# Seventeen unread products, four split loads and two moved steps in the tail of an adaLN decode block

## The chip, the cores and the metric

The kernel runs on one core of a Trainium2 chip. Its metric is the device time of one execution in microseconds. A profile of one execution shows the engines TensorE (PE, with its weight loads as PEld), VectorE (DVE), ScalarE (ACT), GpSimd (POOL) and SyncE (SP, which issues the loads here).

## The reference

Two tokens (B = 2, one position each, D = 512) go through a transformer block in float32: attention over a window of 4,096 cached positions and a feed-forward layer with SiLU, both modulated by a condition c.

```python
x = A_x
mod = (_silu(c) @ w_mod).reshape(c.shape[0], 6, 1, -1)
sa, ca, ga, sb, cb, gb = (mod[:, 0], mod[:, 1], mod[:, 2], mod[:, 3], mod[:, 4], mod[:, 5])
h = _layernorm(x, axis=-1) * (1 + ca) + sa
x = x + ga * _A_ref(h, A_k_cache, A_v_cache, A_wq, A_wo)   # 32 heads, 8 kv heads, Dh 128, then @ wo
h = _layernorm(x, axis=-1) * (1 + cb) + sb
x = x + gb * _B_ref(h, B_w1, B_w2)                         # silu(h @ w1) @ w2, F = 1792
```

## The kernel before, in words

Nearly all of the work is reading: 97.5 MB of caches and weights, for two tokens. SyncE issues all large loads in one queue, in the order in which they are used: w_mod, wq, then a K and a V block of 4 MB each for the eight steps of attention (two kv heads of one token a step), then wo, w1 and w2. They go into four slots of 32 KB per partition in one large tile called `store` (the profile shows all of them under that name), and a load waits until the readers of its slot are done.

Attention (`scores`, `probabilities`, `values`) isn't touched. When it ends, `oTn` (line 443) holds the heads' outputs, turned so that they can be the weights of a product; the big matrices wo, w1 and w2 are always the moving side. Since only two tokens are computed, a product uses 32 columns of weights and writes 32 of PSUM's 128 partitions. Four such products, on the four quarters (`32 * g`), are written one after the other. A matrix row index `q` (32 of them for wo), `k` (4 for w1) or `tt` (14 for w2) stands for 128 rows of the matrix, as `load_rows` (line 402) lays them out: it loads rows `lo` to `hi` of each partition.

The tail, around which the change is made, goes like this:

- **wo** (lines 459 to 476). For rows 0 to 23, quarter `g` takes every fourth row and 512 columns ("wide"), into `acc`. The four partial sums then have to be added: `gather` (line 447) copies them to SBUF on ScalarE (`acc_o_sb`) and multiplies with `id4`. Rows 24 to 31 are "narrow": each of the four quarters takes 128 of the 512 columns of the same row, straight into `ao`. The gather stands behind row 27.
- **The second norm** (lines 477 to 495). VectorE turns `ao`, applies the gate `ga` and the residual, and sums to `ks`; a product with the constant matrix `mean512` gives the mean (`mean_b`, line 488); VectorE makes `dT`, `hT` (the weights for w1) and `vs`. The variance (`var_b`, line 509) is a product with `mean512` as well; ScalarE takes its root.
- **w1** (lines 496 to 513): 16 products of 448 columns into `hid`, row by row, the variance behind row 1.
- **SiLU** (lines 514 to 530): `hidT`, the factor `rstd`, an Exp on ScalarE, and `uT`, the weights for w2.
- **w2** (lines 531 to 552): rows 0 to 7 wide into `acc_yw`, rows 8 to 13 narrow into `acc_y`, a gather behind row 10.
- **Output** (lines 553 to 557): gate `gb`, residual, and one store.

Instructions run on each engine in the order in which a scheduler of the tile framework has put them. What is wrapped in `inorder` (line 63) keeps its place in the program; before, only the attention was wrapped. PSUM tiles come from `bank(tag, name)` (line 68): tags A, B and D have two buffers each, C and O one. A new tile in a buffer waits until those that used it are done, by semaphores.

Of the kernel before, what the change touches and what calls it, by code (L numbers as in the profile page):

```python
# [8 lines left out]
F32 = mybir.dt.float32  # L9
AF = mybir.ActivationFunctionType  # L10
# [3 lines left out]
P = 128  # L14
B, D = 2, 512
# [5 lines left out]
T2 = F // P  # L21
# [5 lines left out]
def adaln_block(  # L27
# [19 lines left out]
    nc = tc.nc  # L47
# [12 lines left out]
    once = ctx.enter_context(tc.tile_pool(name="once", bufs=1))  # L60
    psum = ctx.enter_context(tc.tile_pool(name="psum", bufs=2, space=bass.MemoryType.PSUM))
    psum1 = ctx.enter_context(tc.tile_pool(name="psum1", bufs=1, space=bass.MemoryType.PSUM))
    inorder = tc.keep_in_program_order

    def const(shape, name):
        return consts.tile(shape, F32, name=name)

    def bank(tag, name):
        return (psum1 if tag in "CO" else psum).tile([P, 512], F32, tag=tag, name=name)
# [35 lines left out]
    def summed(shape, name, pattern, axis=AX.X, **sizes):  # L105
        t = const(shape, name)
        nc.vector.tensor_reduce(t, ident.rearrange(pattern, **sizes), axis=axis, op=ALU.add)
        return t

    id4 = summed([P, 32], "id4", "p (a r) -> p r a", r=32)  # L110
# [39 lines left out]
    mean512 = const([P, P], "mean512")  # L150
# [3 lines left out]
    eps_t = const([P, 1], "eps_t")  # L154
# [4 lines left out]
    qbd = [const([P, 4, B, 4, 32], f"qbd{n}") for n in range(2)]  # L159
# [4 lines left out]
    oTn = const([P, 32, 32], "oTn")  # L164
# [3 lines left out]
    hT, uT = const([P, 4, 32], "hT_b"), const([P, T2, 32], "uT")  # L168
# [49 lines left out]
    for s0, s1, m in ((0, 2, m_a), (2, 6, m_b)):  # L218
        for k in range(4):
            v = wm[:, k].rearrange("p (s g m) -> p g s m", s=6, g=4)  # L220
            for g in range(4):
# [4 lines left out]
                    start=(k == 0),  # L226
                    stop=(k == 3),
# [10 lines left out]
    for k in range(4):  # L238
        for n in range(2):
            wv = wqt[:, k].rearrange("p (n s g m) -> p n g s m", n=2, s=4, g=G)  # L240
            for g in range(G):
# [4 lines left out]
                    start=(k == 0),  # L246
                    stop=(k == 3),
# [154 lines left out]
    def load_rows(w, per, lo, hi, s, at):  # L402
        e = w.shape[1]
        n = (hi - lo) * e
        nc.sync.dma_start(s[:, at : at + n], w.rearrange("(p q) e -> p (q e)", q=per)[:, lo * e : hi * e])
        v = s[:, at : at + n].rearrange("p (q e) -> p q e", e=e)
        return {q: v[:, q - lo, :] for q in range(lo, hi)}

    wot, w1t, w2t = {}, {}, {}
    for lo, hi, s, at in ((0, 16, 2, 0), (16, 24, 3, 0), (24, 32, 3, 4096)):  # L410
        wot |= load_rows(wo, 32, lo, hi, slot[s], at)
    for lo, hi in ((0, 2), (2, 3), (3, 4)):
        w1t |= load_rows(w1, 4, lo, hi, slot[0], lo * F)
    WIDE = 8
    for lo, hi in ((0, WIDE), (WIDE, 12), (12, 13), (13, 14)):
        w2t |= load_rows(w2, T2, lo, hi, slot[1], lo * D)

    gaT, sbT, cbT, xT = turned(ga, "gaT"), turned(sb, "sbT"), turned(cb1, "cbT"), turned(x_sp, "xT")
# [4 lines left out]
    for hp in range(HP):  # L423
# [4 lines left out]
            start=True,  # L428
            stop=True,
# [14 lines left out]
        oTn[:, :, 0:32:16], on.rearrange("p b j r -> p r b j"), axis=AX.X, op=ALU.add  # L444
    )

    def gather(acc, wide, name, start, stop):
        sb_ = once.tile([P, D], F32, tag="wide", name=name)
        nc.scalar.copy(sb_, wide)
        for g in range(4):  # L450
            nc.tensor.matmul(
                acc[32 * g : 32 * g + 32, :],
                id4,
                sb_[:, g * P : (g + 1) * P],
                start=start,
                stop=stop,
            )

    acc = bank("D", "acc_o")
    ao = bank("A", "ao")[:, :P]  # L460
    for q in range(24):
        g = q % 4
        nc.tensor.matmul(  # L463
            acc[32 * g : 32 * g + 32, :], oTn[:, q, :], wot[q], start=(q < 4), stop=(q >= 20)
        )
    for q in range(24, 32):
        for g in range(4):
            nc.tensor.matmul(  # L468
                ao[32 * g : 32 * g + 32, :],
                oTn[:, q, :],  # L470
                wot[q][:, g * P : (g + 1) * P],
                start=(q == 24),
                stop=(q == 31),
            )
        if q == 27:
            gather(ao, acc, "acc_o_sb", False, False)
    aoT = once.tile([P, 4, 32], F32, tag="aoT", name="aoT")
    nc.vector.transpose(aoT, ao.rearrange("p (m k) -> p k m", k=4))  # L478
    x1T = once.tile([P, 4, B], F32, tag="x1T", name="x1T")
# [5 lines left out]
    ks = once.tile([P, B], F32, tag="ks", name="ks")  # L485
    nc.vector.tensor_reduce(ks, x1T.rearrange("p k b -> p b k"), axis=AX.X, op=ALU.add)
    mean = bank("B", "mean_b")
    nc.tensor.matmul(mean[:, :B], mean512, ks, start=True, stop=True)
    dT = once.tile([P, 4, B], F32, tag="dT", name="dT")
    nc.vector.tensor_sub(dT, x1T, mean[:, None, :B].to_broadcast([P, 4, B]))  # L490
    nc.vector.tensor_mul(hT[:, :, 0:32:16], dT, cbT[:, :, 0:32:16])  # L491
# [2 lines left out]
    vs = once.tile([P, B], F32, tag="vs", name="vs")  # L494
    nc.vector.tensor_reduce(vs, sq.rearrange("p k b -> p b k"), axis=AX.X, op=ALU.add)
    FC = F // 4
    hp = bank("A", "hid")[:, :FC]
    for k in range(4):
        for g in range(4):
            nc.tensor.matmul(  # L500
                hp[32 * g : 32 * g + 32, :],
                hT[:, k, :],
                w1t[k][:, g * FC : (g + 1) * FC],
                start=(k == 0),
                stop=(k == 3),
            )
        if k == 1:
            var = bank("B", "var_b")
            nc.tensor.matmul(var[:, :B], mean512, vs, start=True, stop=True)
            std = once.tile([P, B], F32, tag="stdb", name="std_b")  # L510
            nc.scalar.activation(std, var[:, :B], AF.Sqrt, bias=eps_t)
            rstd = once.tile([P, B], F32, tag="rstdb", name="rstd_b")
            nc.vector.reciprocal(rstd, std)
    ax = once.tile([P, P], F32, tag="ax", name="ax")
    nc.vector.tensor_mul(ax, ao, ga)
    nc.vector.tensor_add(x1, x_sp, ax)
# [13 lines left out]
    nc.vector.tensor_mul(uT[:, :, 0:32:16], z, sg)  # L530
    yw = bank("D", "acc_yw")
    for tt in range(WIDE):
        g = tt % 4
        nc.tensor.matmul(  # L534
            yw[32 * g : 32 * g + 32, :],
            uT[:, tt, :],
            w2t[tt],
            start=(tt < 4),
            stop=(tt >= WIDE - 4),
        )  # L540
    y = bank("D", "acc_y")[:, :P]
    for tt in range(WIDE, T2):
        for g in range(4):
            nc.tensor.matmul(
                y[32 * g : 32 * g + 32, :],
                uT[:, tt, :],
                w2t[tt][:, g * P : (g + 1) * P],
                start=(tt == WIDE),
                stop=(tt == T2 - 1),
            )  # L550
        if tt == 10:
            gather(y, yw, "acc_y_sb", False, False)
    yo = once.tile([P, P], F32, tag="yo", name="yo")
    nc.vector.tensor_mul(yo, y, gb)
    nc.vector.tensor_add(yo, yo, x1)
# [29 lines left out]
```

## Time and profile before

| | |
|---|---|
| time, median of 3 runs | 238.48 us (238.08 to 238.54) |
| time of the profiled execution | 238.67 us |
| its span, first to last instruction | 236.9 us |
| TensorE busy | 143.4 us (61%) |
| VectorE busy | 113.1 us (48%) |
| ScalarE busy | 28.8 us (12%) |
| mean granted TensorE clock | 0.827 |
| HBM read | 97.53 MB, 412 GB/s over the span |

The profile is of one execution, with times from the start of its span. The chain of waits follows the work that ended last back from the end, at each step to what released it. The timeline gives start, length and kind of merged pieces of one engine, and in brackets how long the engine had been idle and what ended that. Shapes are partitions x elements; "128*32" is the weights' shape. A float32 product shows as two TensorE records. The windows view gives, for each stretch, its length, the busy time of PE, PEld, DVE, ACT and POOL (with the number of records), TensorE's granted clock (1.00 is full), the share of the load engines that was busy, and GB/s.

### The profile page before, as it was taken

What the parts mean: (1) busy time and instruction counts of PE and PEld (TensorE: products, weight loads), DVE (VectorE), ACT (ScalarE), POOL (GpSimd) and SP (SyncE); (2) the same over time, 40 slices, a digit from 0 to 9 for tenths busy, and PEclk for the clock granted to TensorE, in tenths of its full rate; (3) what the DMA queues carried; (4) which work ended last, traced back from release to release, by engine and by line L of the source; (5) the groups of instructions that cost most, each with busy time, mean ns of one, the idle gap of its engine ahead of it and who ended that gap; (6) DMA issues with size and microseconds to landing.
All of it is one profiled execution on the core that took longest, in us unless ns stands there. A gap on an engine that the chain in (4) does not pass through costs nothing.

```text
span 236.9 us, 2420 instructions
## 1 busy us (share of the span) xinstructions
PE 143.4 (61%) x1012; PEld 40.2 (17%) x1012; DVE 113.1 (48%) x155; ACT 28.8 (12%) x64; POOL 7.1 (3%) x27
## 2 busy tenths in 40 slices
PE   0005954638167866887375747737746597736954
PEld 0003211110010211222101200200220222205212
DVE  0125110478497793995394396377449410102130
ACT  2010000010310120111201200300210112030200
POOL 5004000100000000000000000000000000000000
PEclk9999996756957797797979976977997869996579
DMA  7999999999999999999999999999999999999970
GB/s 266 466 421 443 437 418 421 437 415 437 443 433 443 434 409 437 415 429 443 437 432 443 412 437 421 426 443 434 427 437 426 432 423 426 418 421 413 437 300 3
DMA packets 4222, 97.68 MB, mean 412 GB/s; under 512 B 476, under 2 KB 500, under 8 KB 1012
## 3 DMA queue, kind: packets, MB, share of 16 engines
q1 hardware_dynamic: 4188, 97.52, 96.3%
q8 instruction: 8, 0.13, 0.2%
q14 instruction: 2, 0.02, 0.0%
q10 hardware_dynamic: 24, 0.01, 0.0%
HBM read 97.53 MB, written 0.00 MB: 412 GB/s over the span
## 4 chain that ended last, share of the span: by engine, by line
DMA 53%; DVE 24%; PE 12%; issue 6%; ACT 2%; SPq 0%; POOL 0%; ACTq 0%; POOLq 0%
DMA store<-in_A_k_cache_dram 25%; DVE kT L287 17%; DMA store<-in_A_wq_dram 16%; DMA store<-in_A_wo_dram 12%; PE hid L500 2%; PE q L242 2%; PE s L292 2%; DVE store L329 2%; PE acc_yw L534 2%; PE ao L468 1%; ACT store L322 1%; DVE store L327 1%; DVE mx L300 1%; DVE qT L253 1%; ACT L322 1%
## 5 line engine op out<-in xcount | busy, mean ns | idle before, releaser
L287 DVE STREAM_TRANSPOSE kT<-store 128x2048 f32<-128x2048 f32 x32 | 71.1, 2280 | 15.6 <-DMA store<-in_A_k_cache_dram 15.6
L292 PE MATMUL s<-kT,qbd 128*32 128x512 f32 x256 | 48.5, 840 | 31.0 <-DVE kT L287 31.0
L355 PE MATMUL o<-store 128*32 128x512 f32 x256 | 36.8, 725 | 1.0 <-ACT store L345 1.0
L292 PEld LDWEIGHTS s<-kT,qbd 128*32 128x32 f32 x256 | 6.4, 125 | 67.7 <-DVE kT L287 66.9
L242 PE MATMUL q<-store,hq_T 128*32 128x512 f32 x64 | 9.8, 765 | 5.9 <-DMA store<-in_A_wq_dram 5.9
L355 PEld LDWEIGHTS o<-store 128*32 128x32 f32 x256 | 9.3, 129 | 21.4 <-issue 19.8
L327 DVE STREAM_TRANSPOSE store<-store 128x512 f32<-128x512 f32 x8 | 5.7, 711 | 13.5 <-ACT store L322 13.5
L321 ACT COPY bias<-bp 128x1 f32<-128x1 f32 x8 | 1.3, 160 | 89.1 <-PE bp L319 89.1
L187 PE MATMUL mean_a<-mv_a,avg 128*128 128x1 f32 x2 | 0.6, 362 | 18.8 <-DVE avg L112 18.8
L300 DVE TENSOR_REDUCE mx<-s 128x1 f32<-128x512 f32 x8 | 5.5, 692 | 11.2 <-PE s L292 11.2
L329 DVE TENSOR_TENSOR store<-store,half 128x512 f32<-128x512 f32 x16 | 10.4, 689 | 0.2
L336 PE MATMUL pT<-store,sel 128*32 128x256 f32 x64 | 7.5, 414 | 4.5 <-DVE store L329 4.5
L365 PE MATMUL o_all<-store,pick 128*32 128x256 f32 x32 | 7.7, 382 | 2.9 <-ACT store L362 2.9
L362 ACT COPY store<-o 128x512 f32<-128x512 f32 x8 | 4.7, 587 | 31.0 <-PE o L355 31.0
L345 ACT ACTIVATE store<-pT,par 128x256 f32<-128x256 f32 x16 | 6.7, 475 | 10.8 <-PE pT L336 10.8
L253 DVE STREAM_TRANSPOSE qT<-q 128x512 f32<-128x512 f32 x2 | 1.4, 718 | 13.3 <-PE q L242 13.0
L463 PE MATMUL acc_o<-store,oTn 128*32 128x512 f32 x48 | 5.6, 595 | 2.8 <-DMA store<-in_A_wo_dram 2.8
L302 PE MATMUL mT<-ident,mx 128*1 128x128 f32 x16 | 3.0, 270 | 6.5 <-DVE mx L300 6.5
L478 DVE STREAM_TRANSPOSE aoT<-ao 128x128 f32<-128x128 f32 x1 | 0.3, 318 | 13.6 <-PE ao L468 13.6
L438 DVE TENSOR_TENSOR on<-o_all,rq 128x256 f32<-128x256 f32 x1 | 0.4, 425 | 12.3 <-PE o_all L365 12.3
L319 PE MATMUL bp<-negscale,mrow 1*128 1x1 f32 x16 | 3.1, 261 | 5.1 <-DVE mrow L314 5.1
L500 PE MATMUL hid<-store,hT_b 128*32 128x448 f32 x32 | 5.8, 865 | 0.5 <-DVE hT_b L491 0.5
(121 smaller groups left out, 92.9 us busy)
## 6 DMA issues: line engine op xcount, KB each, us to landing
store<-in_A_k_cache_dram SPq DMA_DIRECT2D x8, 4096.0 KB, 29.9
store<-in_A_v_cache_dram SPq DMA_DIRECT2D x8, 4096.0 KB, 28.4
store<-in_A_wq_dram SPq DMA_DIRECT2D x2, 4096.0 KB, 31.8
store<-in_w_mod_dram SPq DMA_DIRECT2D x1, 6144.0 KB, 17.2
store<-in_A_wo_dram SPq DMA_DIRECT2D x1, 4096.0 KB, 32.6
store<-in_A_wo_dram SPq DMA_DIRECT2D x2, 2048.0 KB, 25.1
store<-in_B_w_dram SPq DMA_DIRECT2D x1, 2048.0 KB, 29.1
store<-in_B_w_dram SPq DMA_DIRECT2D x1, 1792.0 KB, 26.2
```

The costliest lines, as they stand in the source:

```text
L242: nc.tensor.matmul(q_ps[n][32 * g : 32 * g + 32, :], hq_T[:, k, :], wv[:, n, g], start=(k == 0), stop=(k == 3),)
L287: inorder(nc.vector.transpose(kT, kv[:, :, j, :]))
L292: inorder(nc.tensor.matmul(s_ps[r : r + 32, :], qbd[h // 4][:, h % 4, b, j, :], kT[:, 32 * f : 32 * f + 32, u:32:2], start=(j == 0), stop= ...
L300: inorder(nc.vector.tensor_reduce(mx, s_ps, axis=AX.X, op=ALU.max))
L327: inorder(nc.vector.transpose(xp, pr))
L329: inorder(nc.vector.tensor_mul(zp[:, 32 * f : 32 * f + 32, :].rearrange("p (s y) w -> p s y w", y=2), xp[:, :, None, 0:16].to_broadcast([P ...
L336: inorder(nc.tensor.matmul(tp[32 * a : 32 * a + 32, :], sel, zp[:, :, 4 * a : 4 * a + 4], start=True, stop=True,))
L345: inorder(nc.scalar.activation(pt[:, :, u, :], tp.rearrange("p (n g) -> p n g", g=G), AF.Copy, scale=par[:, u : u + 1],))
L355: inorder(nc.tensor.matmul(o_ps[32 * c_ : 32 * c_ + 32, :], ptb[t % 2][:, 32 * i : 32 * i + 32], vt[t][:, 512 * i : 512 * i + 512], start= ...
L365: inorder(nc.tensor.matmul(o_all[32 * hp : 32 * hp + 32, :, :], pick[:, n].rearrange("p w i -> p (w i)"), ob[:, :, n, :], start=(n == 0), ...
L463: nc.tensor.matmul(acc[32 * g : 32 * g + 32, :], oTn[:, q, :], wot[q], start=(q < 4), stop=(q >= 20))
L500: nc.tensor.matmul(hp[32 * g : 32 * g + 32, :], hT[:, k, :], w1t[k][:, g * FC : (g + 1) * FC], start=(k == 0), stop=(k == 3),)
```

## The change

Four things are changed, all in the tail.

1. wo's rows 24 to 31 come in two loads instead of one (24 to 27 and 28 to 31), and so do w2's rows 0 to 7 (0 to 3 and 4 to 7).
2. wo's gather stands ahead of rows 28 to 31 in the written order (`copied`, then `narrow` with `id4`), and w2's stands ahead of all the narrow rows. The variance's product with what ScalarE and VectorE make of it stands ahead of w1's first row.
3. `fill(n)` issues n products of `mean512` (128 x 128) with 512 columns of `qbd[0]`, left over from attention, into tiles named "unread" in bank C, which nothing reads: three ahead of wo's rows 28 to 31, two behind them, one behind the mean, three ahead of w1's row 0, two behind its row 2, five behind its row 3, one ahead of w2's gather.
4. All products of the tail go through `product`, which keeps them in program order.

```diff
-    for lo, hi, s, at in ((0, 16, 2, 0), (16, 24, 3, 0), (24, 32, 3, 4096)):
+    for lo, hi, s, at in ((0, 16, 2, 0), (16, 24, 3, 0), (24, 28, 3, 4096), (28, 32, 3, 6144)):
...
-    for lo, hi in ((0, WIDE), (WIDE, 12), (12, 13), (13, 14)):
+    for lo, hi in ((0, 4), (4, WIDE), (WIDE, 12), (12, 13), (13, 14)):
...
+    idle_w = qbd[0].rearrange("p s b j c -> p (s b j c)")[:, :D]
+
+    def fill(n):
+        for _ in range(n):
+            inorder(nc.tensor.matmul(bank("C", "unread"), mean512, idle_w, start=True, stop=True))
+
+    def product(acc, w, rows, g, n, start, stop):
+        inorder(nc.tensor.matmul(
+            acc[32 * g : 32 * g + 32, :n], w, rows, start=start, stop=stop
+        ))
+
+    def narrow(acc, w, rows, start, stop):
         for g in range(4):
...
+            product(acc, w, rows[:, g * P : (g + 1) * P], g, P, start, stop)
+
+    def copied(wide, name):
+        t = once.tile([P, D], F32, tag="wide", name=name)
+        nc.scalar.copy(t, wide)
+        return t
...
     for q in range(24):
...
+        product(acc, oTn[:, q, :], wot[q], q % 4, D, q < 4, q >= 20)
+    acc_sb = copied(acc, "acc_o_sb")
+    for q in range(24, 28):
+        narrow(ao, oTn[:, q, :], wot[q], q == 24, False)
+    narrow(ao, id4, acc_sb, False, False)
+    fill(3)
+    for q in range(28, 32):
+        narrow(ao, oTn[:, q, :], wot[q], False, q == 31)
+    fill(2)
...
-    nc.tensor.matmul(mean[:, :B], mean512, ks, start=True, stop=True)
+    inorder(nc.tensor.matmul(mean[:, :B], mean512, ks, start=True, stop=True))
+    fill(1)
...
+    var = bank("B", "var_b")
+    inorder(nc.tensor.matmul(var[:, :B], mean512, vs, start=True, stop=True))
...
+    fill(3)
     hp = bank("A", "hid")[:, :FC]
     for k in range(4):
         for g in range(4):
...
+            product(hp, hT[:, k, :], w1t[k][:, g * FC : (g + 1) * FC], g, FC, k == 0, k == 3)
+        if k == 2:
+            fill(2)
+    fill(5)
...
     for tt in range(WIDE):
...
+        product(yw, uT[:, tt, :], w2t[tt], tt % 4, D, tt < 4, tt >= WIDE - 4)
+    yw_sb = copied(yw, "acc_y_sb")
     y = bank("D", "acc_y")[:, :P]
+    fill(1)
+    narrow(y, id4, yw_sb, True, False)
     for tt in range(WIDE, T2):
...
+        narrow(y, uT[:, tt, :], w2t[tt], False, tt == T2 - 1)
```

More of the change, by code (lines that the diff above doesn't have):

```diff
@@ L445, in adaln_block @@
     )
-    def gather(acc, wide, name, start, stop):
-        sb_ = once.tile([P, D], F32, tag="wide", name=name)
-        nc.scalar.copy(sb_, wide)
-        for g in range(4):
[L451 to L457, printed above, removed]
+    idle_w = qbd[0].rearrange("p s b j c -> p (s b j c)")[:, :D]
[7 more added lines that the diff above has]
+    def narrow(acc, w, rows, start, stop):
+        for g in range(4):
+            product(acc, w, rows[:, g * P : (g + 1) * P], g, P, start, stop)
[3 more added lines that the diff above has]
+        return t
     acc = bank("D", "acc_o")
@@ L461, in adaln_block @@
     for q in range(24):
[L462 to L476, printed above, removed]
+        product(acc, oTn[:, q, :], wot[q], q % 4, D, q < 4, q >= 20)
[7 more added lines that the diff above has]
+    fill(2)
     aoT = once.tile([P, 4, 32], F32, tag="aoT", name="aoT")
@@ L496, in adaln_block @@
     FC = F // 4
+    var = bank("B", "var_b")
+    inorder(nc.tensor.matmul(var[:, :B], mean512, vs, start=True, stop=True))
+    std = once.tile([P, B], F32, tag="stdb", name="std_b")
+    nc.scalar.activation(std, var[:, :B], AF.Sqrt, bias=eps_t)
+    rstd = once.tile([P, B], F32, tag="rstdb", name="rstd_b")
+    nc.vector.reciprocal(rstd, std)
+    fill(3)
     hp = bank("A", "hid")[:, :FC]
@@ L499, in adaln_block @@
         for g in range(4):
[L500 to L513, printed above, removed]
+            product(hp, hT[:, k, :], w1t[k][:, g * FC : (g + 1) * FC], g, FC, k == 0, k == 3)
+        if k == 2:
+            fill(2)
+    fill(5)
     ax = once.tile([P, P], F32, tag="ax", name="ax")
@@ L532, in adaln_block @@
     for tt in range(WIDE):
[L533 to L540, printed above, removed]
+        product(yw, uT[:, tt, :], w2t[tt], tt % 4, D, tt < 4, tt >= WIDE - 4)
+    yw_sb = copied(yw, "acc_y_sb")
     y = bank("D", "acc_y")[:, :P]
+    fill(1)
+    narrow(y, id4, yw_sb, True, False)
     for tt in range(WIDE, T2):
[L543 to L552, printed above, removed]
+        narrow(y, uT[:, tt, :], w2t[tt], False, tt == T2 - 1)
     yo = once.tile([P, P], F32, tag="yo", name="yo")
```

## The prediction

> **What bounds the kernel now.** I read the chain of waits first. Until 213.7 us it is the loads: caches and weights come in at 412 GB/s over the span, and the change touches nothing of that. The question is the tail. Its rows in the chain (start, length, what):
>
> ```profile
> 213.78 1.25 PE ao L468 x32
> 215.03 0.43 PE ao L451 x8
> 215.46 1.73 PE ao L468 x32
> ...
> 218.32 0.04 issue
> 218.36 0.60 PE mean_b L488 x2
> ...
> 219.41 3.22 PE hid L500 x16
> 222.63 0.52 PE var_b L509 x2
> 223.15 2.52 PE hid L500 x16
> ...
> 227.85 0.22 DVE uT L530
> ...
> 228.16 3.65 PE acc_yw L534 x16
> ...
> 231.89 0.59 ACT acc_y_sb L449
> ...
> 232.53 0.43 PE acc_y L451 x8
> 232.96 0.70 PE acc_y L544 x24
> ...
> 233.68 0.30 DVE yo L554
> ```
>
> TensorE and VectorE hand over to each other from 213.78 to the first yo at 233.68. What follows (the second yo, the store, the end) is unchanged; so whatever moves the start of yo moves the span. The windows view, cut where the clock changes, gives TensorE's clock (the seventh column, the share granted) beside its busy time:
>
> ```profile
> 207.73:211.15 3.42, 1.92 (x16) 0.50 (x16) 0.00 (x0) 0.14 (x1) 0.00 (x0) 1.00 0.97 412
> 211.15:214.56 3.41, 0.78 (x28) 0.78 (x32) 0.00 (x0) 1.73 (x2) 0.00 (x0) 1.00 1.02 432
> 214.56:217.97 3.41, 2.61 (x52) 2.15 (x44) 0.76 (x5) 0.00 (x0) 0.00 (x0) 0.50 0.96 400
> 221.39:224.80 3.41, 3.41 (x22) 1.09 (x18) 0.17 (x1) 1.54 (x2) 0.00 (x0) 0.50 1.01 428
> 228.22:231.63 3.41, 3.41 (x20) 1.05 (x24) 0.00 (x0) 0.00 (x0) 0.00 (x0) 0.50 0.42 160
> ```
>
> The clock changes only in steps of 3.41 us. A stretch with 1.92 us of work left it full, one with 0.78 us dropped it to half for the next, one with 2.61 us did not raise it, a full one did. So hid and acc_yw, the two large groups of the tail, run at half clock. Last, when the weights land (the SP queue's issues, and each one's time to landing):
>
> ```profile
> 184.14 29.60 DMA store<-in_A_wo_dram
> 191.80 0.33 SPq L405 DMA_DIRECT2D store<-in_B_w_dram  x1
> store<-in_B_w_dram SPq DMA_DIRECT2D x1, 1792.0 KB, 26.2
> 198.16 0.33 SPq L405 DMA_DIRECT2D store<-in_B_w_dram  x1
> store<-in_B_w_dram SPq DMA_DIRECT2D x1, 2048.0 KB, 29.1
> 208.90 0.33 SPq L405 DMA_DIRECT2D store<-in_B_w_dram  x1
> store<-in_B_w_dram SPq DMA_DIRECT2D x1, 256.0 KB, 22.1
> ```
>
> wo's last rows land at 213.74, w1's first two at 218.0, w2's first eight at 227.26, its last row at 231.0. So two limits lie near each other: TensorE ends at 233.65, and no change to the tail's work can end it before about 231.4 (231.0, four narrow products, a tail of 0.2). At most some 2.2 us are to be had.
>
> **The change part by part: the price of an unread product.** It is a float32 product of 128 x 512 on all 128 rows of PSUM, which before does not have. Nearest rows:
>
> ```profile
> 204.08 3.64 PE L463 MATMUL acc_o<-store,oTn 128*32 128x512 f32 x32 [1.59 <-DMA store<-in_A_wo_dram]
> 208.97 1.92 PE L463 MATMUL acc_o<-store,oTn 128*32 128x512 f32 x16 [1.26 <-DMA store<-in_A_wo_dram]
> 200.57 1.91 PE L365 MATMUL o_all<-store,pick 128*32 128x256 f32 x8 [0.76 <-ACT store L362]
> 194.52 0.65 PE L336 MATMUL pT<-store,sel 128*32 128x256 f32 x8
> 45.59 0.49 PE L261 MATMUL qr<-qg,rep 128*128 128x128 f32 x2 [0.65 <-POOL qg L257]
> ```
>
> All are at full clock; a product is two records. acc_o's 16 and 8 products differ by 1.72 us, so eight cost 1.72 us, 0.215 each, and 0.20 is the tail of a group. But they write four different quarters of PSUM in turn and run side by side. o_all's four products of 256 columns all write the same 32 rows, so they cannot: (1.91 - 0.20)/4 = 0.43 us each. pT's four of 256 columns, on four quarters, take 0.65 - 0.20 = 0.45 us together. One alone takes as long as four side by side; an unread product fills all four quarters by itself, so for 512 columns it costs 2 x 0.43 = 0.86 us. Bounds: 0.215 (as if it shared the array) and 0.86; I take 0.86, since o_all is the row where nothing overlaps. The Trainium skill has a figure that speaks for less: its page "TensorE: Matmul & The Clock Gate", section "Back-to-back issue gap", gives about 131 ns as the sustained spacing of 512-column matmuls, and "FP8 and Floating Point Precision", section "TensorE Precision Notes", counts four passes for true FP32, which makes an estimated 0.52 us; the o_all row disagrees.
>
> Then the wait. All unread products write the same one-buffer bank C, and in the new order each waits for TensorE's own semaphore. On TensorE before, from wo's narrow rows to the mean, then the same place now (id_91 is the gather's weight, mean_115 the constant matrix mean512):
>
> ```order
> L468 MATMUL ao<-store,oTn 32x128 [waits DMAHW7_49]
> L468 MATMUL ao<-store,oTn 32x128 x15
> L451 MATMUL ao<-acc_o_sb,id_91 32x128 [waits Activation_49]
> L451 MATMUL ao<-acc_o_sb,id_91 32x128 x3
> L468 MATMUL ao<-store,oTn 32x128 x16
> L488 MATMUL mean_b<-ks,mean_115 128x2 [waits DVE_49]
> ```
>
> ```order
> L455 MATMUL ao<-acc_o_sb,id_91 32x128 [waits Activation_49]
> L455 MATMUL ao<-acc_o_sb,id_91 32x128 x3
> L452 MATMUL unread<-qbd_125,mean_115 128x512 [waits PE_49] x3
> L455 MATMUL ao<-store,oTn 32x128 [waits DMAHW0_49]
> L455 MATMUL ao<-store,oTn 32x128 x15
> L452 MATMUL unread<-qbd_125,mean_115 128x512 [waits PE_49] x2
> L491 MATMUL mean_b<-ks,mean_115 128x2 [waits DVE_49]
> ```
>
> The gather moved ahead of the second half of the rows, which now wait for a load of their own, and five unread products stand ahead of the mean. The second and later ones of a group wait until the one before is out of the array. The qr row prices that from an empty start: 0.49 us for 128 columns, of which 0.86/4 = 0.215 is streaming, so 0.275 is start and drain; with 0.04 us from a signal to the next start (the issue row at 218.32) 0.315. Bounds: nothing, and the mean's whole 0.60 us, at half clock; qr is nearest in shape and clock. So the first of a group costs 0.86, each further one 1.17; a group of three 3.20, of two 2.03, of five 5.54. All queue in order on TensorE: whatever stands behind them waits.
>
> Now the queue, at full clock throughout: TensorE is never idle long enough, in any 3.41 us, to fall under the 1.92 us that kept it full. wo's rows 24 to 27 land halfway between the two starts 208.97 and 213.78, at 211.38; their 16 narrow products are four times 0.215, 0.86: 212.24. The gather, whose copy I leave where it was, takes 0.21: 212.45. Three unread: 215.65, which is 1.87 past the landing of rows 28 to 31. Those: 216.51, and with the tail 216.71, where before ended at 217.19: 0.48 gained by earlier work and clock. From ao's end to the mean's start VectorE took 1.17 us (217.19 to 218.36), so the mean could start at 217.88. What VectorE did next before:
>
> ```profile
> 218.99 0.16 DVE L490 TENSOR_TENSOR dT<-x1T,mean_b 128x8 f32<-128x8 f32 x1 [0.68 <-PE mean_b L488]
> 219.47 0.16 DVE L495 TENSOR_REDUCE vs<-sq 128x2 f32<-128x8 f32 x1
> ```
>
> But two unread hold TensorE until 218.54. The mean, about 0.3 at full clock (0.28 to 0.60), gives dT at 218.87, 0.12 earlier than before. So the gain is gone here. One unread: 218.69 to 219.55; vs, 0.64 after dT's start, is ready at 219.51; the variance is queued by 219.70. Three unread: 222.90, while hT is ready and w1's first two rows have been there since 218.0. On TensorE before, then now, from there to acc_yw:
>
> ```order
> L500 MATMUL hid<-store,hT_b 32x448 [waits DMAHW0_49,DVE_49]
> L500 MATMUL hid<-store,hT_b 32x448 x7
> L509 MATMUL var_b<-vs,mean_115 128x2 [waits DVE_49]
> L500 MATMUL hid<-store,hT_b 32x448 [waits DMAHW1_49]
> L500 MATMUL hid<-store,hT_b 32x448 x3
> L500 MATMUL hid<-store,hT_b 32x448 [waits DMAHW2_49]
> L500 MATMUL hid<-store,hT_b 32x448 x3
> L534 MATMUL acc_yw<-store,uT 32x512 [waits DMAHW3_49,DVE_49,PE_49]
> ```
>
> ```order
> L502 MATMUL var_b<-vs,mean_115 128x2 [waits DVE_49]
> L452 MATMUL unread<-qbd_125,mean_115 128x512 [waits PE_49] x3
> L455 MATMUL hid<-store,hT_b 32x448 [waits DMAHW1_49]
> L455 MATMUL hid<-store,hT_b 32x448 x7
> L455 MATMUL hid<-store,hT_b 32x448 [waits DMAHW2_49]
> L455 MATMUL hid<-store,hT_b 32x448 x3
> L452 MATMUL unread<-qbd_125,mean_115 128x512 [waits PE_49] x2
> L455 MATMUL hid<-store,hT_b 32x448 [waits DMAHW3_49]
> L455 MATMUL hid<-store,hT_b 32x448 x3
> L452 MATMUL unread<-qbd_125,mean_115 128x512 [waits PE_49] x5
> L455 MATMUL acc_yw<-store,uT 32x512 [waits DMAHW4_49,DVE_49]
> ```
>
> The variance left hid's middle, and ten unread products stand ahead of acc_yw. A hid product at full clock is 0.215 x 448/512 = 0.188. Twelve: 225.16. Two unread: 227.19. Four: 227.94, tail 228.14; before 225.67, so 2.47 late, although hid itself takes 3.0 instead of 5.7. From hid's end to uT VectorE and ScalarE take 2.40 (225.67 to 228.07): uT at 230.54. But five unread last until 233.48, 2.9 past uT. acc_yw, 1.72 and tail, ends at 235.40 instead of 231.81. The copy with its gaps: 236.07; the one unread there ends at 236.06 and is hidden. The gather and 24 narrow products, 0.21 + 1.29 + 0.20: 237.77, yo at 237.80. That is 4.1 us later than 233.68.
>
> The moved variance saves nothing: its Sqrt, table load and rstd end long before hid. The loads: two more issues on SP, each 0.33, and as completion counters are shared in turn, w2's later loads wait in the new program for wo's to land, the last until 213.74. That costs nothing: the load queue ahead of it is then still 17 us long (231.0). If splitting slows the rows, bounded by one issue each, 0.3 us either way, that is covered since acc_yw starts after the last row has landed. The profiled execution took 238.67, 0.19 over the median of 238.48; 4.1 more gives 242.8 for it and **242.6** for a median.
>
> **The rivals.** First, the products fit the gaps: faster. If an unread product streams in 0.43, half my price, then by the same steps (0.74 with the wait) ks is ready before the mean's turn, hid ends at 224.05, uT is ready at 226.45, acc_yw ends at 229.16, and yo waits for w2's last row: 231.56, 2.1 earlier, 236.4. Between the two prices the time moves 6.2 us for 0.43, so the sides change at 0.58 a product. For it: half clock really does cost hid and acc_yw some 5 us before. Against it: the o_all row. By the skill's 0.52 it would be about 0.8 us faster. That the products do not run at all is in this case too: rows and clock alone gain about the same; the order speaks against it. Chance 0.06.
>
> Second, the wait costs nothing, because TensorE overlaps start and drain in spite of the semaphore. With 0.86 for each product the same steps give hid's end at 226.28, acc_yw's at 232.30, yo at 234.69: 1.0 later, 239.5. For it: acc_o's products hide all but one tail; against it: those have no wait between them. Chance 0.14.
>
> Third, the clock falls to half in spite of it all, since with waits the products stream only 0.86 of 1.17, 73%, and 2.61 of 3.41 (77%) did not raise it before. Then every later product doubles, 10 us or more: over 250. Against it: 1.92 of 3.41 kept it full, and it is full when they start. Chance 0.04.
>
> **How the numbers follow.** My forecast has 0.72: TensorE's queue becomes the bound. Prices between the first two rivals that cancel out: 0.04. A measurement can tell about 0.2%, 0.5 us. So faster 0.06, same 0.04, slower 0.72 + 0.14 + 0.04 = 0.90. The range goes down to the second rival, 239.4. Upward, if each of the ten waits costs 0.5 (most of the mean's 0.60), 1.9 more: 244.5. That leaves out the first rival, the third and some edges, under 2 in 10.
>
> **What would show it.** Right: TensorE's clock 1.00 from 211 to the end, unread products about 1.17 us apart, the mean, hid and acc_yw each released by TensorE's own queue and not by VectorE or a load, uT ready almost 3 us before acc_yw starts, yo near 237.8. Wrong: unread products 0.5 us apart, or acc_yw starting when uT or w2's rows arrive.

## The result, and the profile after

The changed kernel takes 245.31 us (median of 6 runs, 245.23 to 245.83), the kernel before 238.25 us (6 runs, 237.91 to 238.54): a ratio of 1.0301, with a 95% interval of 1.0287 to 1.0315. It is 7.1 us slower; forecast were 242.6 us and at most 244.5. The profiled execution took 245.29 us, with a span of 243.5. Its yo starts at 240.05 instead of 233.68, 6.37 us later; the forecast had 237.80.

The chain of waits, from the landing of wo's rows 24 to 27 on (start, length, what):

```profile
211.39 1.30 PE ao L455 x40
212.69 1.07 PE unread L452 x2
213.76 0.04 issue
213.80 1.14 PE unread L452 x2
214.94 0.04 issue
214.99 1.12 PE unread L452 x2
216.11 1.01 PE ao L455 x32
...
219.36 0.12 PE mean_b L491 x2
219.48 1.07 PE unread L452 x2
...
224.10 2.39 PE hid L455 x24
...
228.73 0.89 PE hid L455 x8
...
235.41 1.85 PE acc_yw L455 x16
...
240.05 0.30 DVE yo L542
```

From 211.39 to 240.03 there is nothing but TensorE in it: no load, and neither VectorE nor ScalarE. The unread products follow each other 1.19 us apart (213.80, 214.99), each released by the one before. VectorE has its part ready long before it is wanted; from its timeline, ks and uT:

```profile
218.12 0.16 DVE L489 TENSOR_REDUCE ks<-x1T 128x2 f32<-128x8 f32 x1
231.85 0.20 DVE L531 TENSOR_TENSOR uT<-z,sgh 128x28 f32<-128x28 f32 x1
```

The mean starts about 1.1 us after ks, acc_yw 3.4 us after uT. The windows view (length, busy time by engine, the clock in the seventh column):

```profile
204.50:207.60 3.10, 3.10 (x20) 1.09 (x16) 0.00 (x0) 0.00 (x0) 0.00 (x0) 0.50 0.98 418
211.40:229.50 18.10, 17.75 (x130) 6.68 (x130) 1.79 (x11) 3.27 (x4) 0.00 (x0) 1.00 0.99 411
229.50:235.30 5.80, 5.57 (x14) 1.49 (x10) 1.94 (x7) 0.23 (x1) 0.00 (x0) 1.00 0.09 36
```

The clock is full from 211.40 on, to the end: hid takes 2.39 + 0.89 us where it took 5.7, acc_yw 1.85 where it took 3.65. The price is that TensorE works almost without a pause (17.75 of 18.10 us), and still does so when the loads have ended (36 GB/s in the last row).

### The profile page after: what moved, and what is told of

It reads as the page before. It is cut to its first block, busy times and chain, and to the rows that moved or that the text cites. A ratio compares the mean times of both kernels' runs of the same rounds, so it can differ in the third digit from the quotient of the medians.

```text
span 243.5 us, 2490 instructions
## 1 busy us (share of the span) xinstructions
PE 153.6 (63%) x1046; PEld 42.6 (18%) x1046; DVE 113.2 (46%) x155; ACT 28.8 (12%) x64; POOL 7.1 (3%) x27
## 4 chain that ended last, share of the span: by engine, by line
DMA 60%; DVE 17%; PE 15%; issue 5%; ACT 1%; SPq 0%; POOL 0%; POOLq 0%
DMA store<-in_A_k_cache_dram 34%; DMA store<-in_A_wq_dram 15%; DVE kT L287 14%; DMA store<-in_A_wo_dram 11%; PE unread L452 8%; PE q L242 2%; PE hid L455 1%; PE ao L455 1%; PE acc_yw L455 1%; PE acc_y L455 1%; DVE qT L253 1%; DVE store L329 1%; ACT L322 1%; PE s L292 0%; DVE qbd L267 0%
## 5 line engine op out<-in xcount | busy, mean ns | idle before, releaser
L292 PE MATMUL s<-kT,qbd 128*32 128x512 f32 x256 | 47.8, 823 | 33.2 <-DVE kT L287 33.2
L355 PE MATMUL o<-store 128*32 128x512 f32 x256 | 33.6, 670 | 1.0 <-ACT store L345 1.0
L452 PE MATMUL unread<-qbd,mean 128*128 128x512 f32 x34 | 19.1, 645 | 0.6
L355 PEld LDWEIGHTS o<-store 128*32 128x32 f32 x256 | 8.7, 122 | 19.2 <-issue 17.6
L455 PE MATMUL acc_o<-store,oTn 128*32 128x512 f32 x48 | 7.1, 750 | 3.2 <-DMA store<-in_A_wo_dram 3.2
L452 PEld LDWEIGHTS unread<-qbd,mean 128*128 128x128 f32 x34 | 5.1, 188 | 11.6 <-PE unread L452 8.9
```

What stands on the lines that cost most here:

```text
L292: inorder(nc.tensor.matmul(s_ps[r : r + 32, :], qbd[h // 4][:, h % 4, b, j, :], kT[:, 32 * f : 32 * f + 32, u:32:2], start=(j == 0), stop= ...
L355: inorder(nc.tensor.matmul(o_ps[32 * c_ : 32 * c_ + 32, :], ptb[t % 2][:, 32 * i : 32 * i + 32], vt[t][:, 512 * i : 512 * i + 512], start= ...
L452: inorder(nc.tensor.matmul(bank("C", "unread"), mean512, idle_w, start=True, stop=True))
L455: inorder(nc.tensor.matmul(acc[32 * g : 32 * g + 32, :n], w, rows, start=start, stop=stop))
```

## The experiments

Three sets on three chips, each beside runs of the kernel before on its own chip. Ratios are against those, with a 95% interval; they compare all times of a run, so they are not the ratios of the medians. Only the changed kernel differs from the kernel before by more than 2%. Where a smaller difference is called faster or slower below, it is because its interval leaves out 1.

**e1_none, without the unread products.** This kernel leaves out all seventeen.

```diff
     def fill(n):
-        for _ in range(n):
-            inorder(nc.tensor.matmul(bank("C", "unread"), mean512, idle_w, start=True, stop=True))
+        return
```

> The changed kernel without the seventeen unread products; loads, order and everything that is read are unchanged. Theory (the products, queued on TensorE, are the whole loss): wo's rows 28 to 31 start when they land at 213.8, hid waits for w1 at 218.0 and runs partly at half clock, and yo waits for w2's last rows: 236.1 to 237.0 us, 1.2 to 2.1 faster than before. Rival (split loads, shared completion counters or the new order lose time too): 238.3 us or more.

237.76 us (237.14 to 239.31), ratio 0.9982 (0.9960 to 1.0004). The whole loss is gone, so it lies in the unread products; against the kernel before, loads and order together lose nothing. But the gain is smaller than either figure of the theory, and the times spread over 2.2 us. The profiled execution (237.38 us) shows why there was little to gain. Its chain:

```profile
218.11 5.37 PE hid L454 x32
...
225.98 3.55 PE acc_yw L454 x16
...
232.05 0.30 DVE yo L541
```

ao is done 2.2 us earlier, hid starts when w1 lands, but both large groups run at half clock for most of their time, as before.

**e2_group, without the waits.**

```diff
-        for _ in range(n):
-            inorder(nc.tensor.matmul(bank("C", "unread"), mean512, idle_w, start=True, stop=True))
+        t = bank("C", "unread")
+        for i in range(n):
+            inorder(nc.tensor.matmul(t, mean512, idle_w, start=i == 0, stop=i == n - 1))
```

> As changed, but the unread products of one place are one accumulation in one tile, so that only the first of a group waits. Theory (a further product pays 0.32 us for draining and refilling the array): ten waits fewer, 3.2 us less than the change, 242.1 us. Rival (the wait costs nothing, the product itself is 1.18 us long): 245.3 us as before the experiment.

242.12 us (242.06 to 242.20), ratio 1.0151 (1.0119 to 1.0182): the theory to 0.02 us. Its chain has each group in one piece:

```profile
212.84 2.77 PE unread L453 x6
215.61 1.01 PE ao L456 x32
216.62 1.91 PE unread L453 x4
218.54 0.12 PE mean_b L492 x2
...
227.82 4.49 PE unread L453 x10
232.31 1.85 PE acc_yw L456 x16
...
236.95 0.30 DVE yo L543
```

Three products take 2.77, five 4.49: 0.86 for each further one, as priced from o_all, and a remainder of 0.2 in every group. yo starts 3.10 us earlier than with the waits, although wo's rows 24 to 27 landed 0.15 later in this execution: from that landing on it is 3.25, ten waits of 0.325.

**e3_half, half as many columns, waits kept.**

```diff
-            inorder(nc.tensor.matmul(bank("C", "unread"), mean512, idle_w, start=True, stop=True))
+            inorder(nc.tensor.matmul(bank("C", "unread")[:, :256], mean512, idle_w[:, :256], start=True, stop=True))
```

> As changed, but each unread product has 256 columns instead of 512; the waits stay. Theory (0.86 us of streaming, by columns, plus 0.32 us for a wait): 0.43 us less for each; 0.75 with a wait; the queue still ends about with before: yo near 233.5, 238.1 us. Rival (the cost is mostly fixed per product, not by columns): over 242 us.

238.62 us (238.53 to 238.74), ratio 1.0007 (0.9990 to 1.0024). The products are paid by columns: by its chain, unread products with a wait start 0.76 us apart instead of 1.19. The time is 0.5 us over the theory, but not because of TensorE's queue: yo starts at 233.34 in its profile, 0.16 ahead of the 233.5 expected. The theory added 4.6 us from yo's start to the whole time, and here it is 5.26, as in the changed kernel (5.24). All twelve times lie within 0.21 us, while 26 runs of the kernel before on that chip spread from 237.60 to 239.24.

**e4_loads, the split loads alone, in the kernel before.**

```diff
-    for lo, hi, s, at in ((0, 16, 2, 0), (16, 24, 3, 0), (24, 32, 3, 4096)):
+    for lo, hi, s, at in ((0, 16, 2, 0), (16, 24, 3, 0), (24, 28, 3, 4096), (28, 32, 3, 6144)):
...
-    for lo, hi in ((0, WIDE), (WIDE, 12), (12, 13), (13, 14)):
+    for lo, hi in ((0, 4), (4, WIDE), (WIDE, 12), (12, 13), (13, 14)):
```

> The kernel before with the two load splits alone. Theory (the splits cost nothing and let half of wo's last rows and the gather run before the others land): ao done near 214.9 instead of 217.2, hid starts with w1 at 218.0 instead of 219.4: about 1.4 us faster than before, 236.8 us. Rival (smaller loads and shared counters slow the queue): 238.3 us or more.

237.28 us (237.16 to 237.59), ratio 0.9945 (0.9926 to 0.9964): faster, by 1.0 to the median beside it. Here the scheduler put the variance ahead of hid by itself, and wo's gather between the two halves of the narrow rows, where it had been all along. So of the moved steps only w2's gather was a move beyond what the loads bring. Its chain shows what ends it now:

```profile
208.94 21.02 DMA store<-in_B_w_dram
...
230.09 1.07 PE acc_y L544 x24
...
232.10 0.30 DVE yo L554
```

hid (5.95 us) and acc_yw (3.22 us) still run long here, but acc_yw ends at 229.90 and isn't in the chain any more: the last step waits for w2's rows 8 to 11, which land at 229.96. On the same chip e4 is 0.5 us below e1_none by the median, and its times spread over 0.4 us instead of 2.2, though yo starts at the same point in both profiles (232.10 and 232.05). In e1_none acc_yw, the copy and the gather stand ahead of all narrow rows and are in the chain; that this makes its executions longer is not shown.

**e5_bridge, two unread products alone, behind hid.** The group of e2, everywhere else left out.

```diff
-    fill(3)
...
-    fill(2)
...
-    fill(1)
...
-    fill(3)
...
-        if k == 2:
-            fill(2)
-    fill(5)
+    fill(2)
...
-    fill(1)
```

> The changed kernel's loads and order, with two unread products, as one group, behind hid alone; the other fifteen are left out. Theory (only the gap from hid to uT, 2.5 us in the run without unread products, costs clock: acc_yw took 3.55 us there and would take 1.9): the group ends before uT, acc_yw ends when w2's row 7 has landed plus 1 us, yo near 231.5 instead of 232.05: 236.8 us. Rival (the loads' end leaves nothing to gain, or two products do not hold the clock): 237.3 us or more.

236.98 us (236.88 to 237.16), ratio 0.9957 (0.9941 to 0.9974). From its timeline, the group and the products behind it, which run at full clock (1.00 from 223.30 to 229.00):

```profile
223.31 1.98 PE L453 MATMUL unread<-qbd,mean 128*128 128x512 f32 x4
225.92 1.07 PE L456 MATMUL acc_yw<-store,uT 128*32 128x512 f32 x8 [0.62 <-DVE uT L526]
227.40 1.07 PE L456 MATMUL acc_yw<-store,uT 128*32 128x512 f32 x8 [0.41 <-DMA store<-in_B_w_dram]
229.88 1.70 PE L456 MATMUL acc_y<-store,uT 128*32 128x128 f32 x48 [0.23 <-DMA store<-in_B_w_dram]
231.65 0.29 DVE L536 TENSOR_TENSOR yo<-acc_y,mod_sp 128x128 f32<-128x128 f32 x1 [5.83 <-PE acc_y L456]
```

The group ends 0.6 us before acc_yw may start, acc_yw waits for its own rows, and yo starts 0.40 us earlier than in e1_none's profile. Its w2's last row was issued at 213.8 and landed 17.3 us later, at 231.1, 0.55 us before yo; in e8 below that distance is 0.54. So this is the loads' end. That the two products make the kernel faster than the same loads and order without them isn't shown by the times: the interval overlaps that of e1_none, which ran on another chip. Nor is any run with unread products shown to be faster than e4_loads, which has none (0.9945).

**e6_quarter, the grouped products on narrow weights.**

```diff
-        for _ in range(n):
-            inorder(nc.tensor.matmul(bank("C", "unread"), mean512, idle_w, start=True, stop=True))
+        t = bank("C", "unread")[:, :512]
+        for i in range(n):
+            for g in range(4):
+                product(t, id4, idle_w[:, :512], g, 512, i == 0, i == n - 1)
```

> As the grouped run, but each unread product of 128 columns of weights becomes four of 32 (id4), on the four quarters, side by side: the same 0.86 us of streaming. Theory (what was still missing in the sum, about 2.3 us, is the change between weights of 128 and of 32 columns, 0.2 us into a group and 0.15 us out of it): 239.8 us. Rival (any new group or tile costs it, whatever the width): 242.1 us as the grouped run.

240.78 us (240.72 to 240.92), ratio 1.0116 (1.0093 to 1.0139), between the two. The chain answers line by line to that of e2:

```profile
212.74 2.58 PE unread L457 x24
215.32 0.87 PE ao L457 x32
216.19 1.72 PE unread L457 x16
217.91 0.31 PE mean_b L493 x2
218.22 0.99 PE unread L457 x8
...
226.97 4.29 PE unread L457 x40
231.26 1.72 PE acc_yw L457 x16
...
235.54 0.30 DVE yo L544
```

Now the groups that follow narrow weights take 0.86 a product, and ao and acc_yw after them 0.14 and 0.13 less: the change of width is what cost 0.2 into a group and 0.14 out of it. It isn't any new group or tile, since these are new too. The mean, whose weights are 128 wide, became 0.19 longer in exchange, and so did the variance, and the groups behind these two still pay 0.13 for the way back (0.99 for one product). That is the larger part of why 1.41 us is saved in yo and not 2.3; 0.10 of the 1.41 is that wo's rows landed earlier than in e2. A product on 128 columns of weights also fills all four quarters at once, and e6 changes both together; what in the array takes the time is not shown.

**e7_small and e8_fit, products that fit the gaps.** e7 is e2 with 128 columns, e8 is e6 with 256.

```diff
-        t = bank("C", "unread")
+        t = bank("C", "unread")[:, :128]
...
-            inorder(nc.tensor.matmul(t, mean512, idle_w, start=i == 0, stop=i == n - 1))
+            inorder(nc.tensor.matmul(t, mean512, idle_w[:, :128], start=i == 0, stop=i == n - 1))
```

> As the grouped run, but with 128 columns for 512 in each unread product: 0.215 us of streaming. Theory (groups of 1.0, 0.8, 0.55, 1.0, 0.8 and 1.4 us fit into the gaps, and TensorE keeps full clock): yo waits for w2's last row, 231.4 to 231.7: 236.7 us, with little spread. Rival (so few columns do not hold the clock): 237.3 to 237.8 us with the spread of the run without unread products.

> As the quarter-wide run, but with 256 columns: 0.43 us for four side by side, no wait, no change of width. Theory (at half the price the seventeen fit the gaps, as the first rival of the prediction had it, and w2's last row ends the kernel): 236.7 us, 1.6 us faster than before, with little spread. Rival (TensorE's queue is still too long somewhere): 238 us or more.

e7: 237.03 us (236.84 to 237.53), ratio 0.9959 (0.9942 to 0.9977). e8: 237.15 us (236.96 to 237.29), ratio 0.9968 (0.9952 to 0.9984). Both are faster, as the theory has it, by 0.7 and 0.6 us to the median beside them (237.77). But only e8 keeps TensorE at full clock in the tail: in e7's profile it is at half from 218.24 to 221.65, and hid's first twelve products take 4.07 us, without moving the end. e8's chain ends on w2's last row:

```profile
213.87 17.45 DMA store<-in_B_w_dram
...
231.37 0.47 PE acc_y L457 x8
...
231.86 0.30 DVE yo L544
```

So products at half the price fit the gaps, as the first rival of the prediction had it, when they wait for nothing and stay quarter-wide. At half the price with waits and full-width weights e3 had yo at 233.34 and not at 231.56: the rival's sum, which has the waits, leaves out the same term as the forecast, and the price of 0.58 at which the sides were to change is too high, since e3 at 0.43 is the same as before.

**e9_one_w2 and e10_one_wo, e5 with one of the splits undone.**

```diff
-    for lo, hi in ((0, 4), (4, WIDE), (WIDE, 12), (12, 13), (13, 14)):
+    for lo, hi in ((0, WIDE), (WIDE, 12), (12, 13), (13, 14)):
```

```diff
-    for lo, hi, s, at in ((0, 16, 2, 0), (16, 24, 3, 0), (24, 28, 3, 4096), (28, 32, 3, 6144)):
+    for lo, hi, s, at in ((0, 16, 2, 0), (16, 24, 3, 0), (24, 32, 3, 4096)):
```

> As the run with two unread products behind hid, but w2's rows 0 to 7 in one load, as before the change. Theory (w2's split buys nothing, since rows 4 to 7 land at 227.4 in either case and acc_yw at full clock then takes 1.9 us, ahead of row 8's landing at 229.8 plus what w2's last row needs): 236.7 to 237.0 us, the same or 0.2 us faster, by w2's last row landing at 231.0 instead of 231.2. Rival (the split matters): 237.3 us or more.

> As the run with two unread products behind hid, but wo's rows 24 to 31 in one load, as before the change. Theory (wo's split is what the change has of use: it takes half of the narrow rows and the gather, 1.2 us at full clock, out of the way before the last rows land): ao, the mean and hid 1.2 us or more later, 237.5 to 238.5 us, with the spread of the kernel before, whose clock hangs on where the 3.41 us steps fall. Rival (hid waits for w1 and the end for w2 in any case): 237.0 us.

Both theories fell. e9: 237.41 us (237.13 to 239.64), ratio 0.9982 (0.9955 to 1.0008). e10: 237.11 us (236.79 to 237.78), ratio 0.9951 (0.9931 to 0.9970). wo's split isn't needed for the gain. w2's is worth some 0.3 us to the median of e9 against e10, 0.39 in yo. Without it the gain is only unclear, not gone: nine of e9's twelve times lie below every time of the kernel before on that chip (237.57 and more), three lie between 238.78 and 239.64, and why is not shown. In e9's timeline acc_yw has to wait for all eight rows at once:

```profile
225.79 0.21 DVE L526 TENSOR_TENSOR uT<-z,sgh 128x28 f32<-128x28 f32 x1
227.59 1.92 PE L456 MATMUL acc_yw<-store,uT 128*32 128x512 f32 x16 [2.13 <-DMA store<-in_B_w_dram]
```

and the copy, the gather and 24 narrow products come behind it, to 232.05. I had compared acc_yw's end with a landing and left out what still follows. In e10's profile ao is 2.4 us later than in e5's, but hid, which in e5 had to wait for w1's rows and ran most of its first twelve products at half clock, runs through in 3.52 us and ends at the same time.

## Why the prediction was wrong in size, point by point

**The bound: right.** TensorE's queue became the bound, and the mean, hid and acc_yw were each released by it. That nothing before 231.4 was to be had was right as well: the best yo of all runs is e5's 231.65.

**An unread product streams for 0.86 us: right,** by e2 and e6 (0.86 each) and by e3 (paid by columns). The estimate of 0.52 us, worked out in the prediction from the 131 ns that the Trainium skill's page "TensorE: Matmul & The Clock Gate", section "Back-to-back issue gap", gives for 512 columns, is not borne out by these runs.

**A waited product pays 0.315 us more: right.** They stood 1.19 us apart against 1.17, and taking ten waits away moved yo by 3.10 against 3.15 (3.25 from the landing of wo's rows on). The second rival is out.

**"So the first of a group costs 0.86": this step failed.** A group of one took 1.07 us. The seven groups took 19.26 us by the chain against 17.72, 0.2 too much in each; the quarter-wide groups behind them (ao, hid twice, acc_yw) 0.55 more than priced. That is 2.1 of the 2.25 us that are missing in yo. The rest is the first ao group with its gather, 1.30 us for a price of 1.07 that left out the 0.20 of a group's tail, less 0.06 at the mean and the variance. The last of the seven was to be hidden behind the copy, but ended 0.35 us after it. The prices came from rows in which the width of the weights never changes (acc_o, o_all, pT) or from a product into an idle array (qr), and I put them side by side without a term for the change. e6 shows that it goes with the width. The range failed with it: its upper end stretched only the waits. Of the 2.7 us between 242.6 and 245.31, the other 0.45 is not in the tail's work: 0.25 lies behind yo's start (5.24 us to the end of the time against 4.99 in the profile before), where I had expected no change, and 0.19 was taken off the forecast because the profiled execution before was that much over its median, which after it is not (245.29).

**The clock: right where it counted.** It was full from 211.40 to the end, as forecast. Before that, from 204.50 to 207.60, it was at half, which the sum doesn't contain, but acc_o still ended at 211.14, before wo's next rows landed at 211.35. The third rival, 73% of streaming being too little to hold the clock, is out. The measure behind the forecast, that 1.92 us of work in 3.41 keep it full, does not hold in general: e7 lost it after 2.43 us.

**The gather moved: wrong, without a consequence.** The order quoted in the prediction shows wo's gather between the two halves already; only the load they wait for changed.

**The loads cost nothing: right.** By e4 they even gain 1.0 us, and by the ratios no kernel with unread products gains more. In the changed kernel that gain is buried: split up by the runs, yo is 1.82 us earlier with products that fit (e8 against before), 3.68 later by the full length (e6 against e8), 1.41 by the changes of width that e6 takes away (e2 against e6) and 3.10 by the waits (the changed kernel against e2), which makes the 6.37. The terms are taken from single executions on different chips, whose landings differ by up to 0.15 us.

That the kernel before spreads (236.8 to 239.4 in the three sets) because the clock's steps fall differently on its gaps is argued, not shown: the runs whose tail has no gap spread little (e2 0.14 us, e3 0.21), but each profile is of one execution, and the mean granted clock of the whole execution doesn't go with its time in any of the three sets.

## What to carry to other kernels

Work put into a gap to keep TensorE's clock up has to be priced like any other: columns at the rate of a group that cannot run side by side, the drain where a one-buffer tile makes each product wait for the last, and the change to another width of weights on both sides. Make such a group shorter than the gap, as one accumulation; two products in the one gap ahead of the last large group did as well here as seventeen small ones. But the two split loads without any unread product (e4) did as well as either, since the wait for w2's rows then covers what half clock costs: no run here shows that unread products are worth having in this kernel. And look first at when the loads end: with 2.2 us to be had at most, 14.6 us of extra streaming had nowhere to go.

## What the runs showed of the hardware that was not expected

Going over from weights of 32 columns to weights of 128 cost about 0.2 us, and going back 0.14, at full clock (e2 against e6: groups of three 2.77 and 2.58 us, the narrow products behind them 1.01 and 0.87). And a stretch that is not quite full can raise the clock: in the run e10_one_wo, 2.78 us of work in 3.41 did, where 2.61 had not in the kernel before. Nor does a fixed share keep it up: 1.92 us had left it full in the kernel before, but in e7_small the stretch from 214.83 to 218.24, at full clock, had 2.43 us of work, and the next was at half. So the profile's busy time, in which the ends of products are modelled, doesn't tell by itself when the clock changes.

```profile
214.50:217.91 3.41, 2.78 (x56) 2.32 (x46) 0.59 (x4) 0.00 (x0) 0.00 (x0) 0.50 0.98 408
217.91:221.30 3.39, 2.09 (x20) 1.14 (x24) 1.21 (x8) 1.27 (x2) 0.00 (x0) 1.00 1.00 413
```
